# Reversed column order in the three-pass float32r products of an attention, mixer and mixture kernel

## The chip, the cores and the metric

The kernel runs on one core of a Trainium2 chip. The metric is the device time of one execution in microseconds, as the median of the runs shown. One further execution was taken with the hardware profiler, and all rows below come from it.

## The reference, cut to what matters

Three stages follow one another, for a batch of 4, a sequence of 448 and a model width of 768 (12 heads of 64):

```python
q_n, k_n = rmsnorm(q, g_q), rmsnorm(k, g_k)             # stage 1, per head
attn = softmax(q_n @ k_n.T / 8);  x = attn @ v
h  = relu(x.T @ w_tok1) @ w_tok2                        # stage 2, over the sequence
u  = x + h.T
u  = u + relu(u @ w_ch1) @ w_ch2                        # over the channels, 768 -> 1536 -> 768
for e in range(4):                                      # stage 3, causal attention experts
    ye = softmax(mask(q_e @ k_e.T / 8)) @ v_e @ wo[e]   # q_e, k_e, v_e = u @ wq[e], wk[e], wv[e]
    out += gate_e(u) * ye                               # top 2 of 4 by u @ w_gate
```

All inputs and the output are float32.

## The kernel before, in words

**Two kinds of matrix product.** The score products (line 577), the products with v (line 643) and the transposes (lines 603, 620, 658) take float32 operands. The dense products, which are those with the token weights, the channel weights, the expert projections and the output weights, go through the helpers `product` and `mm3`. There each operand is held as two float32r halves, a rounded one (index 0) and the rest (index 1), side by side in a tile of shape [128, 2, width]. `mm3` multiplies in three passes, (0,0), (1,0) and (0,1) of stationary half and moving half, each one matmul (line 508) that adds to the same row of PSUM. All of these have 128 stationary columns, or 112 for the values of the experts. The moving operand has 448 columns, in 2,304 passes; 260 columns for the values with the gate, in 288; and 256 columns in the first token product, in 288. The output row in PSUM has as many columns and is contiguous, as the moving operand is.

**What feeds and follows them.** A weight tile (`whl`, ring of 6) is split into its halves on ScalarE and VectorE or POOL the first time it is needed, written to a DRAM copy (`kept`) and fetched from there for the later batches (line 499). `narrow` unpacks the raw weights, with reads that take every second 32-bit word (lines 453 and 456, and `half` in 458 and 460). The moving operands `uhl`, `hid`, `xhl` and the second halves are written by ScalarE (lines 419, 424) and VectorE (lines 425, 438, 918, 951). After the last pass of a product ScalarE or VectorE reads the finished PSUM row (lines 419, 424, 934, 951, 962); each reads it by one instruction over the whole row.

**Order of the work.** All steps are collected by a planner (`Plan`) that lays them out on a model of the engines: `product` gives it a cost of three times `pass_ns(n)` for three passes, and the order so found is issued as it is. The two PSUM rows of a ring (`ps_a`, `ps_m`, `ps_s`, two buffers each) and the SBUF rings (`RING`) bound how far it runs ahead. The tags in `SHIFT` get 64 bytes of padding ahead of their ring. Attention pairs of one batch are interleaved with the dense products of the batch before, so that ScalarE's exponentials and VectorE's row maxima (lines 562 and 552) have TensorE work beside them.

Of the kernel before, what the change touches and what calls it, by code (L numbers as in the profile page):

```python
# [308 lines left out]
def kernel(  # L309
# [196 lines left out]
    def mm3(acc, lhs, rhs, first, last):  # L506
        for i, (x, y) in enumerate(PASSES):
            nc.tensor.matmul(  # L508
                acc, lhs[:, x], rhs[:, y], start=first and i == 0, stop=last and i == 2
            )  # L510

    def product(acc, pa, terms, n, more=False):

        m = len(terms)
        for i, (reads, lhs, rhs) in enumerate(terms):
            add("PE", 3 * pass_ns(n), reads, [pa],
                lambda i=i, lhs=lhs, rhs=rhs: mm3(
                    acc(), lhs(), rhs(), i == 0, i == m - 1 and not more))
# [632 lines left out]
```

## Time and profile before

| what | value |
|---|---|
| median of 3 runs | 908.91 us (907.31 to 909.79) |
| span of the profiled execution | 903.5 us (its page gives no other time of its own) |
| TensorE matmul busy | 874.8 us, 97% |
| weight load busy (overlaps the matmuls) | 690.0 us, 76% |
| VectorE, ScalarE, POOL busy | 527.4, 441.7, 55.1 us |
| data moved by DMA | 163.28 MB, 181 GB/s |

The span runs from the first to the last instruction; a timed run is some microseconds longer. A matmul's duration in the rows is that of one instruction from its start to the end of its results, and matmuls overlap, so the time of a stream of them is read from the starts: the time between two starts, divided by the number of matmuls between.

### The profile page before, as it was taken

How to read it: one execution, taken by the hardware profiler on the slowest of the kernel's cores; microseconds unless marked ns; L12 is line 12 of the kernel's file. 1: busy time of each engine (PE TensorE's matmuls, PEld its weight loads, DVE VectorE, ACT ScalarE, POOL GpSimd, SP SyncE). 2: the span in 40 equal slices, each digit the busy share in tenths (PEclk: the TensorE clock that was granted, in tenths of full speed). 3: DMA queues.
4: the chain of work that ended last, by engine and by line, in shares of the span. 5: the costliest groups of instructions: out<-in, count | busy, mean ns of one | idle time of the engine just before them, and what ended most of it. 6: DMA issues, size and time to landing. Idle time of an engine off the chain costs nothing.

```text
span 903.5 us, 14257 instructions
## 1 busy us (share of the span) xinstructions
PE 874.8 (97%) x5160; PEld 690.0 (76%) x5160; DVE 527.4 (58%) x1154; ACT 441.7 (49%) x1047; POOL 55.1 (6%) x68
## 2 busy tenths in 40 slices
PE   3899999999999999999999999999999999999998
PEld 1445688777778878868778787887777799998886
DVE  7998999899984964453452574443363282124342
ACT  5898856767763553344244345144434440004453
POOL 1014001020100200000000010000000010001000
PEclk9999999999999999999999999999999999999999
DMA  7755868787779538846355406764453225675334
GB/s 203 199 172 171 236 222 270 246 264 261 240 261 246 171 108 243 255 150 206 104 161 148 157 21 177 223 209 156 121 169 109 62 80 175 222 232 173 111 128 169
DMA packets 103223, 163.28 MB, mean 181 GB/s; under 512 B 14096, under 2 KB 70288, under 8 KB 103152
## 3 DMA queue, kind: packets, MB, share of 16 engines
q1 hardware_dynamic: 103008, 162.36, 58.2%
q8 instruction: 41, 0.67, 0.3%
q14 instruction: 30, 0.25, 0.1%
q10 hardware_dynamic: 144, 0.00, 0.0%
HBM read 131.55 MB, written 30.77 MB: 180 GB/s over the span
## 4 chain that ended last, share of the span: by engine, by line
PE 87%; DVE 5%; ACT 5%; DMA 1%; issue 1%; ACTq 0%; DVEq 0%; SPq 0%
PE a L508 56%; PE s L577 10%; PE m L643 9%; PE s L620 7%; PE m L658 3%; ACT s L562 2%; DVE nm L552 1%; DMA nat<-in_nat_dram 1%; PE s L582 1%; PE a L603 1%; ACT s L419 1%; DVE st L755 1%; ACT wraw L453 0%; ACT w L456 0%; DVE s L420 0%
## 5 line engine op out<-in xcount | busy, mean ns | idle before, releaser
L508 PE MATMUL a<-uhl,whl 128*128 128x448 f32 x1152 | 246.4, 366 | 1.1 <-DVE whl L438 0.6
L508 PEld LDWEIGHTS a<-uhl,whl 128*128 128x128 f32 x1152 | 212.5, 188 | 27.9 <-issue 9.4
L508 PE MATMUL a<-hid,whl 128*128 128x448 f32 x864 | 190.1, 368 | 0.0
L562 ACT ACTIVATE s<-s,nm,st 112x448 f32<-112x448 f32 x192 | 137.2, 726 | 101.5 <-DVE nm L556 59.9
L508 PEld LDWEIGHTS a<-hid,whl 128*128 128x128 f32 x864 | 158.2, 188 | 22.9 <-issue 9.5
L552 DVE TENSOR_REDUCE nm<-s 112x2 f32<-112x896 f32 (+3 forms) x128 | 125.9, 998 | 73.0 <-PE s L577 40.3
L577 PE MATMUL s<-k,q 64*112 64x448 f32 (+3 forms) x512 | 109.7, 543 | 5.7 <-ACT s L562 4.9
L419 ACT ACTIVATE s<-s 112x896 f32<-112x896 f32 (+3 forms) x121 | 78.9, 696 | 53.3 <-PE s L620 49.4
L962 DVE TENSOR_TENSOR u<-a,u 128x448 f32<-128x448 f32 x72 | 44.6, 622 | 72.6 <-PE a L508 72.2
L620 PE MATMUL s<-ident,s 112*112 112x112 f32 x736 | 81.9, 259 | 0.0
L620 PEld LDWEIGHTS s<-ident,s 112*112 112x112 f32 x736 | 75.0, 133 | 5.3 <-issue 0.7
L424 ACT ACTIVATE hid<-a 128x448 fp32r<-128x448 f32 x42 | 22.9, 544 | 112.6 <-PE a L508 112.5
L643 PE MATMUL m<-s,v 112*64 112x448 f32 x384 | 77.2, 545 | 0.0
L577 PEld LDWEIGHTS s<-k,q 64*112 64x112 f32 x512 | 39.6, 177 | 46.0 <-issue 28.7
L951 DVE SCALAR_TENSOR_TENSOR hid<-a,hid 128x448 fp32r<-128x448 f32 x48 | 29.8, 622 | 75.8 <-ACT hid L424 75.8
L643 PEld LDWEIGHTS m<-s,v 112*64 112x64 f32 x384 | 25.5, 136 | 41.5 <-issue 39.5
L562 ACT ACTIVATE s<-s,nm 112x112 f32<-112x112 f32 (+3 forms) x64 | 30.9, 493 | 39.7 <-DVE nm L552 39.4
L562 ACT ACTIVATION_READ_ACCUMULATOR s<-s,nm,st 112x1 f32 x192 | 39.3, 204 | 0.0
L508 PE MATMUL a<-whl,uhl 128*112 128x260 f32 x288 | 39.0, 287 | 0.0
L508 PE MATMUL a<-xhl,t 112*128 112x256 f32 x288 | 37.9, 284 | 0.6 <-ACT s L419 0.3
L508 PEld LDWEIGHTS a<-whl,uhl 128*112 128x112 f32 x288 | 35.5, 175 | 2.2 <-issue 1.4
L508 PEld LDWEIGHTS a<-xhl,t 112*128 112x128 f32 x288 | 34.8, 188 | 2.8 <-issue 1.4
(123 smaller groups left out, 906.5 us busy)
## 6 DMA issues: line engine op xcount, KB each, us to landing
whl<-kept_c SPq DMA_DIRECT2D x72, 384.0 KB, 4.1
whl<-kept_c SPq DMA_DIRECT2D x108, 256.0 KB, 3.2
w<-in_wc_dram SPq DMA_DIRECT2D x24, 384.0 KB, 4.1
kept_c<-whl SPq DMA_DIRECT2D x24, 384.0 KB, 4.1
w<-in_wc_dram SPq DMA_DIRECT2D x36, 256.0 KB, 3.2
kept_c<-whl SPq DMA_DIRECT2D x36, 256.0 KB, 3.7
whl<-kept_qk SPq DMA_DIRECT2D x24, 384.0 KB, 3.5
nat<-in_nat_dram SPq DMA_DIRECT2D x19, 448.0 KB, 4.6
```

What stands on the lines that cost most here:

```text
L419: lambda e: nc.scalar.activation(dst(), src(), AF.Copy) if e == "ACT"
L424: lambda e: nc.scalar.activation(dst(), src(), AF.Relu) if e == "ACT"
L508: nc.tensor.matmul(acc, lhs[:, x], rhs[:, y], start=first and i == 0, stop=last and i == 2)
L552: lambda e: e.tensor_reduce(nm.t[:, c], pst.t[:CP, :, :w], axis=AX.X, op=ALU.max, negate=True))
L562: lambda j=j: nc.scalar.activation(s[j].t[:, c, :w], pst.t[:CP, j, :w], AF.Exp, bias=nm.t[:, c, j : j + 1], scale=1.0 if rq is None else r ...
L577: nc.tensor.matmul(pst.t[:CP, j, :w], q.t[me, CP * c : CP * c + CP], k.t[me, :w], start=True, stop=not causal)
L582: nc.tensor.matmul(pst.t[:CP, j, width[c] - CP : width[c]], eye, veil, start=False, stop=True)
L620: nc.tensor.transpose(pst.t[:CP, c - cc, CP * r : CP * r + CP], s.t[:, r, CP * c : CP * c + CP], ident[:CP, :CP])
L643: nc.tensor.matmul(av.t[64 * j : 64 * j + 64, q0:S], vat(j, c)[1](), p.t[:, c, q0:], start=c == 0, stop=c == NCH - 1)
L658: nc.tensor.transpose(dst(c), src(c), ident[:p, :p])
L951: lambda e, hl=hl, pa=pa: e.scalar_tensor_tensor(hl.t[:, 1], pa.t[:, :S], 0.0, f(hl.t[:, 0]), op0=ALU.max, op1=ALU.subtract))
L962: dve(S, [pa], [u], lambda e, u=u, pa=pa: e.tensor_add(u.t, pa.t[:, :S], u.t))
```

## The change

Both the moving operand and the PSUM row of `mm3` are given with a step of minus one in the column dimension. The last column is read first and written first, to the last place of the row, so every column's sum goes where it went. The stationary operand, the order of the passes, the flags, all other matmuls, the planner and its costs stay.

```diff
     def mm3(acc, lhs, rhs, first, last):
         for i, (x, y) in enumerate(PASSES):
             nc.tensor.matmul(
-                acc, lhs[:, x], rhs[:, y], start=first and i == 0, stop=last and i == 2
+                acc[:, ::-1], lhs[:, x], rhs[:, y][:, ::-1],
+                start=first and i == 0, stop=last and i == 2,
             )
```

## Rows read from the trace of the kernel before

**Rows 1.** The page, busy time of each engine: us (share of the span) xinstructions.
```profile
PE 874.8 (97%) x5160; PEld 690.0 (76%) x5160; DVE 527.4 (58%) x1154; ACT 441.7 (49%) x1047; POOL 55.1 (6%) x68
```
**Rows 2.** The page, chain that ended last: shares by engine, then by line.
```profile
PE 87%; DVE 5%; ACT 5%; DMA 1%; issue 1%; ACTq 0%; DVEq 0%; SPq 0%
...
PE a L508 56%; PE s L577 10%; PE m L643 9%; PE s L620 7%; PE m L658 3%; ACT s L562 2%; DVE nm L552 1%; DMA nat<-in_nat_dram 1%; PE s L582 1%; PE a L603 1%; ACT s L419 1%; DVE st L755 1%; ACT wraw L453 0%; ACT w L456 0%; DVE s L420 0%
```
**Rows 3.** Windows, all instructions: window, length, busy of five engines, PEclk, DMA share, GB/s.
```profile
0.00:25.00 25.00, 9.42 (x31) 3.69 (x32) 19.25 (x51) 14.75 (x32) 3.14 (x10) 0.93 0.67 191
...
150.00:300.00 150.00, 149.44 (x882) 113.19 (x880) 123.44 (x289) 98.49 (x242) 17.50 (x18) 1.00 0.82 258
...
660.00:800.00 140.00, 140.00 (x823) 119.85 (x822) 53.69 (x118) 38.91 (x85) 3.86 (x5) 1.00 0.46 144
```
**Rows 4.** Waits of PE for other engines: total us, times, longest (three longest of 14).
```profile
PE m L658 <- DVE st L758: 9.8, 1, 9.8
PE s L577 <- ACT s L562: 4.9, 4, 2.9
PE a L603 <- ACT s L419: 2.3, 8, 0.6
```
**Rows 5.** PE in order of time, 740.8 to 817: start, us, operation xcount.
```profile
743.24 14.56 PE L508 MATMUL a<-uhl,whl 128*128 128x448 f32 x72
757.64 14.56 PE L508 MATMUL a<-hid,whl 128*128 128x448 f32 x72
772.04 14.56 PE L508 MATMUL a<-uhl,whl 128*128 128x448 f32 x72
786.44 14.56 PE L508 MATMUL a<-hid,whl 128*128 128x448 f32 x72
800.84 14.56 PE L508 MATMUL a<-uhl,whl 128*128 128x448 f32 x72
```
**Rows 6.** PE in order of time, the narrow passes and what starts after them.
```profile
280.08 4.58 PE L508 MATMUL a<-whl,uhl 128*112 128x260 f32 x36
284.49 0.74 PE L620 MATMUL s<-ident,s 112*112 112x112 f32 x6
...
304.40 1.65 PE L508 MATMUL a<-xhl,t 112*128 112x256 f32 x12
305.88 0.83 PE L620 MATMUL s<-ident,s 112*112 112x112 f32 x7
```
**Rows 7.** Line 508 by itself: duration min/median/max ns of matmuls and weight loads.
```profile
L508 PEld LDWEIGHTS a<-uhl,whl x1152: 186/188/192, 118.0 to 859.6; 128*128 128x128 f32 x192
L508 PE MATMUL a<-uhl,whl x1152: 360/363/476, 118.0 to 859.8; 128*128 128x448 f32 x192
```
**Rows 8.** Chain in order of time: one float32 product with v, 8 matmuls in 16 records.
```profile
34.48 3.16 PE m L643 x16
```
**Rows 9.** ScalarE groups: reads of every second word (L453), then contiguous reads (L419).
```profile
L453 ACT ACTIVATE wraw<-w 128x384 f32<-128x384 f32 x24 | 13.4, 559 | 5.5 <-DMA w<-in_wc_dram 3.7 <-DVE nm L552 1.8
...
L419 ACT ACTIVATE whl<-wraw 128x384 fp32r<-128x384 f32 x10 | 5.4, 536 | 8.6 <-DVE wraw L460 6.0 <-PE a L508 2.6
```

## The prediction

> **What bounds the kernel now.** The first view is the busy time of the engines: TensorE's matmuls are busy for 874.8 of 903.5 us, and no other engine passes 58% [rows 1]. The second is the chain that ended last: 87% of it is TensorE, and line 508 alone, the three-pass products, is 56%, some 506 us [rows 2]. The third are windows along the span: from about 150 us on TensorE is busy for practically every microsecond, also where the DMA engines have their highest share (149.44 of 150 us beside a DMA share of 0.82); only the first 25 us, which hold no line 508 work worth counting, are a stage of waits on others [rows 3]. The largest wait of a matmul for another engine is 9.8 us, once, on the statistics at the start; the next is 4.9 us in four pieces [rows 4]. So TensorE's own rate is the bound. What a pass of line 508 gains or loses reaches the end nearly one to one, and the only question is what a pass costs with its columns in the other order.
>
> That cost is read from the starts in an undisturbed stretch near the end. Seventy-two passes begin at 743.24 and the next seventy-two at 757.64: 14.40 us / 72 = 200.0 ns per pass of 448 columns, and the same in each of the four intervals [rows 5]. The granted clock there is 1.00, so 2.4 GHz [rows 3]; one column per cycle would be 448 / 2.4 = 186.7 ns. A pass thus takes 13.3 ns beyond its columns. For the narrow passes: 36 of 260 columns from 280.08 to 284.49, 122.5 ns each against 108.3 for the columns alone; 12 of 256 columns from 304.40 to 305.88, 123.3 ns against 106.7, each with the turn to another kind of work in it [rows 6]. The stream is limited by columns; the weight load, 188 ns each, fits under a pass of 200 [rows 7].
>
> **The change part by part.** No instruction is added, removed or moved. The planner's costs aren't touched, so the issue order, the DMAs, the rings and the waits stay. The two halves of a moving operand stay apart in the reversed form, and the consumers read whole rows after the last pass, so it is of no use or harm to them which column was written first. What changes is the inside of 2,304 + 288 + 288 = 2,880 matmuls: the order in which TensorE reads SBUF and writes PSUM.
>
> 1. *The moving read, step minus one.* The trace has no negative step on any engine. Nearest row: ScalarE reading every second word of 384 takes 559 ns against 536 for contiguous words, 4% more [rows 9]. That instruction is slower per column than TensorE, so it shows only that a step other than one isn't punished by itself. The lower end is a gain of all that a pass has beyond its columns: 13.3 x 2,304 = 30.6 us, 14.2 x 288 = 4.1 us and 16.6 x 288 = 4.8 us, together 39.5 us. The upper end: each column takes twice its time. The nearest row for a matmul that handles 448 columns at such a rate is the float32 product with v, 8 matmuls in 3.16 us or 395 ns each [rows 8]. By it a pass costs 195 ns more: 195 x 2,304 = 449 us; a narrow pass of about 258 columns would be 395 x 258 / 448 = 227 ns, 104 more than its 123, x 576 = 60 us; together 509 us.
> 2. *The PSUM write, step minus one.* Read and write run in the same stream, so the slower sets the pass; the ends are the same two, and they are not added.
>
> I take 0 for both. The reversed stream touches the same words, four bytes apart, one neighbour after the other, and the one row with another step is 4% from the contiguous one, far nearer to none than to twice. The sum by the profiled execution is 903.5 + 0 = 903.5 us of span. The runs' median lies 908.91 - 903.5 = 5.4 us above that span; this part (start and end of an execution) isn't touched, so the forecast is 908.9 us. What this kernel's timing can tell from no change is about 0.3%, 2.7 us; shared over 2,880 passes that is 0.95 ns per pass. The forecast of no change is therefore a narrow one: a pass between 199.1 and 200.9 ns.
>
> The rule that speaks against the change is the Trainium skill's, in Advanced Engine Details and Errata, section Memory Cachelines: SBUF is accessed in lines of 16 bytes and PSUM in lines of 8, two float32 values, and a non-contiguous pattern in PSUM slows matmuls markedly. If a descending row counts as non-contiguous there, the sum would be the one of the second rival below; if only the line counts, two neighbours in descending order still share one and the sum stays. No run here shows which.
>
> **The rivals.**
>
> *A. A pass gets shorter, and the kernel faster.* The 13.3 ns beyond the columns may be cycles in which the moving read and the read of the next weights, which runs at the same time in SBUF, disturb each other. Reversing one of the two streams alters how they meet. For it: weight loads are busy beside the matmuls for 76% of the span [rows 1]. Against it: nearly the same excess stands on passes of 448, 260 and 256 columns (13.3, 14.2, 16.6 ns) [rows 5, 6], which looks like a fixed step per matmul, and a step like that doesn't care for the order. All of it gone is 39.5 us: 869.4 us; half of it 889 us. With TensorE faster, the next thing late would be the weight fetches in the 150 to 300 us window, where the DMA engines are already at 0.82 [rows 3]; 7% less time would put them at 0.88, still under the whole. The skill's page TensorE: Matmul & The Clock Gate, section Step-by-step, gives the weights and the moving operand two separate read ports of SBUF, so that a weight load takes nothing from the running matmul; by that the gain would be 0. The trace doesn't contradict it and doesn't prove it.
>
> *B. Each column takes twice its time (slower).* Place: the PSUM write, or the SBUF read, of the 2,880 passes. If neighbours are only taken together in ascending order, a reversed row is handled one column at a time. Point from which it decides: at 2.4 GHz a column has 0.42 ns; as soon as one descending column needs more, every pass is bound by it, and nothing hides it, since TensorE is the bound already. Price as in part 1: 509 us, or 908.9 + 509 = 1,418 us by the nearest row; by exact doubling of the columns (186.7 x 2,304 + 107.5 x 576 = 492 us) 1,401 us. Against it stands only that the words are neighbours all the same; no row of a reversed operand speaks for or against.
>
> *C. The same disturbance as in A, but more of it (slower).* If the order makes the two streams meet more often, an excess that doubles costs what A would win: 908.9 + 39.5 = 948 us, half of that 929 us.
>
> *D. The change doesn't do what it says:* a matmul with a reversed operand runs in the slower float32 form, with its operands taken twice. At two matmul records for each pass, as line 643 has, and each column at twice its time, it would be far past B, some 2 x 395 = 790 ns per pass of 448 columns, above 2,200 us. Nothing in the profile speaks for it.
>
> **How the numbers follow.** No change within 0.3%: 0.43. A: 0.20, most of it near half of the excess. C: 0.14. B: 0.20. D: 0.03. Faster is A, 0.20; within 0.3% is 0.43; slower is B, C and D, 0.37. Cases of both signs and one with a price of half the kernel hold most of the chance together, so the range is wide: it leaves out D, and the part of A in which over 60% of the excess goes, and reaches up to B's price: 884 to 1,420 us. The likeliest case has a range of its own of 906.2 to 911.6 us.
>
> **What would show each step.** In the profile of the changed kernel I expect the five starts of the long stretch again 14.40 us apart for 72 passes, the median matmul at 363 ns, the weight load at 188 ns, the matmuls' busy share at 97%, and the same count of instructions. Under A or C those intervals move by up to 0.96 us per 72 while the float32 lines (577, 620, 643) keep their durations, and the excess changes more on rows of 448 than on 256. Under B they become 27 to 28 us, line 508 rises from 56% of the chain to over 70%, and VectorE and ScalarE fall below 40% and 33% of a span of 1,400 us at unchanged busy time. Under D line 508 has twice its records. The prediction is wrong if a pass of the long stretch differs from 200.0 ns by over 1 ns, or if a wait appears at line 508 that rows 4 don't have, such as on the second half of `hid`.

## The result, and the profile after

The changed kernel takes 919.54 us (918.92 to 921.79, 4 runs) against 908.11 us (906.15 to 909.79, 4 runs) for the kernel before: a ratio of 1.0134, with a 95% interval of 1.0114 to 1.0155. It is slower by about 11.4 us. The forecast was no change, 908.9 us. The direction is that of rival C, at a little over half of C's smaller price.

The page after, busy time of the engines, against rows 1:

```profile
PE 887.8 (97%) x5160; PEld 691.7 (75%) x5160; DVE 527.9 (58%) x1154; ACT 442.9 (48%) x1047; POOL 54.8 (6%) x68
```

The counts are the same on every engine. TensorE's matmuls are busy for 13.0 us more, and no other row here moved by more than 1.7 us. TensorE in order of time in the long stretch, against rows 5:

```profile
753.98 15.04 PE L508 MATMUL a<-uhl,whl 128*128 128x448 f32 x72
768.86 15.04 PE L508 MATMUL a<-hid,whl 128*128 128x448 f32 x72
783.74 15.04 PE L508 MATMUL a<-uhl,whl 128*128 128x448 f32 x72
798.62 15.04 PE L508 MATMUL a<-hid,whl 128*128 128x448 f32 x72
813.50 15.04 PE L508 MATMUL a<-uhl,whl 128*128 128x448 f32 x72
```

The starts are 14.88 us apart in each of the four intervals, so 206.7 ns a pass where [rows 5] gave 200.0. The granted clock there is 1.00 again, as the windows after show (columns as in rows 3):

```profile
660.00:800.00 140.00, 140.00 (x818) 117.17 (x815) 56.19 (x125) 43.54 (x95) 3.83 (x5) 1.00 0.42 132
```

Line 508 by itself, against rows 7, and then the 260-column passes in order of time, against rows 6:

```profile
L508 PEld LDWEIGHTS a<-uhl,whl x1152: 186/188/192, 118.9 to 873.5; 128*128 128x128 f32 x192
L508 PE MATMUL a<-uhl,whl x1152: 366/368/476, 118.9 to 873.7; 128*128 128x448 f32 x192
```

```profile
283.56 4.57 PE L508 MATMUL a<-whl,uhl 128*112 128x260 f32 x36
287.97 1.12 PE L621 MATMUL s<-ident,s 112*112 112x112 f32 x10
```

A matmul of 448 columns lasts 368 ns and not 363; the weight load still lasts 188 ns; the 36 passes of 260 columns again take (287.97 - 283.56) / 36 = 122.5 ns.

Where the time went can be added up, since both kernels issue the same matmuls in the same order. From the first to the last matmul start the trace before spans 889.7 us and the trace after 903.4 us, 13.6 us more. Of these, 2,173 intervals between two successive passes of 448 columns hold 12.2 us (5.6 ns each in the mean; those at a turn between kinds of work change less), 269 intervals between passes of 256 columns hold 0.5 us (2.0 ns each), 269 of 260 columns hold 0.0 us, and the longer gaps beside all these under 1 us. The first matmul starts 0.6 us later. That makes the 14.2 us between the spans of 917.7 and 903.5 us. The medians lie 11.4 us apart: the run whose span is 917.7 us took 919.54 us, 1.8 us more, so the profiled execution of before would have been a run of about 905.3 us, faster than its median.

The largest wait of a matmul is still the one at the start:

```profile
PE m L659 <- DVE st L759: 10.4, 1, 10.4
```

### The profile page after: what moved, and what is told of

The parts are those of the page before. It is cut to its first block, busy times and chain, and to the rows that moved or that the text cites. A ratio compares the mean times of both kernels' runs of the same rounds, so it can differ in the third digit from the quotient of the medians.

```text
span 917.7 us, 14271 instructions
## 1 busy us (share of the span) xinstructions
PE 887.8 (97%) x5160; PEld 691.7 (75%) x5160; DVE 527.9 (58%) x1154; ACT 442.9 (48%) x1047; POOL 54.8 (6%) x68
## 4 chain that ended last, share of the span: by engine, by line
PE 85%; DVE 5%; ACT 4%; DMA 4%; issue 1%; SPq 0%; ACTq 0%; DVEq 0%
PE a L508 55%; PE s L578 10%; PE m L644 9%; PE s L621 7%; PE m L659 3%; ACT s L563 2%; DMA nat<-in_nat_dram 1%; DMA rs<-st 1%; PE a L604 1%; PE s L583 1%; DVE nm L553 1%; ACT s L419 1%; DMA whl<-kept_c 1%; DMA out_dram<-ot 0%; DVE st L756 0%
## 5 line engine op out<-in xcount | busy, mean ns | idle before, releaser
L508 PE MATMUL a<-uhl,whl 128*128 128x448 f32 x1152 | 253.3, 372 | 1.0 <-ACT ot L419 0.4
L508 PE MATMUL a<-hid,whl 128*128 128x448 f32 x864 | 195.1, 373 | 0.5 <-DMA whl<-kept_c 0.5
L419 ACT ACTIVATE s<-s 112x896 f32<-112x896 f32 (+3 forms) x121 | 78.8, 696 | 55.8 <-PE s L621 51.9
L578 PEld LDWEIGHTS s<-k,q 64*112 64x112 f32 x512 | 39.5, 176 | 46.1 <-issue 28.2
L458 DVE SCALAR_TENSOR_TENSOR wraw<-wraw,w 128x256 uint32<-128x256 uint32 (+3 forms) x72 | 32.9, 457 | 8.2 <-ACT w L456 5.5
```

The source lines that it names most:

```text
L419: lambda e: nc.scalar.activation(dst(), src(), AF.Copy) if e == "ACT"
L458: dve(n, [(d, 0)], [(r, part)], lambda e: e.scalar_tensor_tensor(ru(), ru(), 3, half(0), op0=ALU.logical_shift_left, op1=ALU.bitwise_or), ...
L508: nc.tensor.matmul(acc[:, ::-1], lhs[:, x], rhs[:, y][:, ::-1], start=first and i == 0, stop=last and i == 2,)
L578: nc.tensor.matmul(pst.t[:CP, j, :w], q.t[me, CP * c : CP * c + CP], k.t[me, :w], start=True, stop=not causal)
```

## The experiments

**One side of the change at a time.** In the first only the moving read is reversed, in the second only the PSUM write.

```diff
-                acc[:, ::-1], lhs[:, x], rhs[:, y][:, ::-1],
+                acc, lhs[:, x], rhs[:, y][:, ::-1],          # e1
+                acc[:, ::-1], lhs[:, x], rhs[:, y],          # e2
```

> Only the moving operand is read from its last column to its first; the PSUM row is written first to last, so each product's columns come out mirrored (its time is what is asked for). Theory R (the extra time arises where the moving operand is read from SBUF, beside the read of the next weights): a pass of 448 columns takes the changed kernel's 206.7 ns, 72 passes 14.88 us, the whole about 919.5 us. Theory W (it arises where the row is written to PSUM, for instance because two neighbours are only taken together in ascending order): 200.0 ns, 14.40 us, the whole about 908 us. If both sides share in it: between the two.

> Only the PSUM row is written from its last place to its first; the moving operand is read first to last, so each product's columns come out mirrored. Theory R: 200.0 ns a pass, 14.40 us for 72, the whole about 908 us. Theory W: 206.7 ns, 14.88 us, about 919.5 us.

TensorE in order of time in the same stretch, first with the reversed read, then with the reversed write:

```profile
770.27 15.04 PE L508 MATMUL a<-hid,whl 128*128 128x448 f32 x72
785.15 15.04 PE L508 MATMUL a<-uhl,whl 128*128 128x448 f32 x72
800.03 15.04 PE L508 MATMUL a<-hid,whl 128*128 128x448 f32 x72
```

```profile
758.68 14.56 PE L508 MATMUL a<-hid,whl 128*128 128x448 f32 x72
773.08 14.56 PE L508 MATMUL a<-uhl,whl 128*128 128x448 f32 x72
787.48 14.56 PE L508 MATMUL a<-hid,whl 128*128 128x448 f32 x72
```

With the read alone the intervals are 14.88 us and the time is 918.53 us, a ratio of 1.0128 (1.0098 to 1.0157). With the write alone they are 14.40 us and the time is 906.9 us, a ratio of 1.0008 (0.9995 to 1.0022). Theory W falls: the whole of the loss belongs to the moving read, and a PSUM row written from its last place to its first costs nothing that can be measured.

**All weights from one column.** The 128 stationary columns are read from one word of each partition (step zero), ascending (e3) and descending (e4).

```diff
-                acc, lhs[:, x], rhs[:, y], start=first and i == 0, stop=last and i == 2
+                acc, lhs[:, x][:, 0:1].to_broadcast(list(lhs[:, x].shape)), rhs[:, y],
+                start=first and i == 0, stop=last and i == 2,
```

> The kernel before (both ascending), with the 128 stationary columns all read from the first column of their block (step zero), so that the weight load touches one word per partition and not 128; the products are not those of the reference. Theory R, in the form that the moving read and the weight read disturb each other in SBUF: the 13.3 ns beyond the columns shrink, a pass falls below 195 ns (186.7 to 190 if all of it is from there) and the whole below 896 us. A fixed step of each matmul, or theory W: 200 ns stays, the whole about 908 us.

> The changed kernel (both descending) with the same one-column weight load as the run before it; the products are not those of the reference. Theory R in the form of a disturbance between the two reads: the excess of the reversed order goes with it, a pass takes what the ascending one takes in that run, below 195 ns. If the 6.7 ns belong to a descending stream by itself, read or write: 6.7 ns above the ascending run with one weight column, so about 194 to 197 ns, or 206.7 ns if the weight read has no part in any of it.

The same stretch, ascending and then descending:

```profile
765.08 15.04 PE L508 MATMUL a<-hid,whl 128*128 128x448 f32 x72
779.96 15.07 PE L508 MATMUL a<-uhl,whl 128*128 128x448 f32 x72
794.87 15.04 PE L508 MATMUL a<-hid,whl 128*128 128x448 f32 x72
```

```profile
765.15 14.88 PE L508 MATMUL a<-hid,whl 128*128 128x448 f32 x72
779.87 14.88 PE L508 MATMUL a<-uhl,whl 128*128 128x448 f32 x72
794.59 14.88 PE L508 MATMUL a<-hid,whl 128*128 128x448 f32 x72
```

None of the expectations was met. The ascending kernel got slower (14.88 to 14.91 us, 207 ns; 915.53 us in one run beside 906.43 us) and the descending one a little faster than the changed kernel (14.72 us, 204.4 ns; 914.79 us). But the moving operand, its order and its place are the same as in the kernel before (e3) or the changed one (e4), and only the words that the weight load reads differ. So the weight read does act on the pass, and fewer words touched didn't help. Whether it acts by where it reads or by its step of zero, these two runs can't tell.

**Other places.** If place counts, the padding of `SHIFT` matters: it puts the weights 64 bytes, counted modulo 128, from the start of the moving operand, in all passes with `uhl` or `hid` as moving operand and `whl` as weights. The profile holds no addresses: this distance, here and below, is worked out from where the program's buffers lie, from the lowest address of the moving operand to the weights that are loaded during the pass. Two runs spread the six weight buffers by 32 bytes each (four floats are asked for, and the buffers end up 32 bytes further apart) and move `hid` as well:

```diff
-SHIFT = {"t1", "h1", "uhl"}
+SHIFT = {"t1": 16, "h1": 16, "uhl": 16, "hid": 24}
...
-            self.tile = self.pool.tile(
-                self.shape, self.dtype, tag=self.tag, name=self.name, bufs=self.bufs
-            )
+            flat = self.tag == "whl"
+            self.tile = self.pool.tile(
+                [128, 768 + 4] if flat else self.shape,
+                self.dtype, tag=self.tag, name=self.name, bufs=self.bufs
+            )
+            if flat:
+                self.tile = self.tile[:, :768].rearrange("p (h k) -> p h k", h=2)
```

> The kernel before with the six buffers of the weight ring 32 bytes further apart each and the ring of hid moved by 96 bytes more, so that the distance in SBUF between the moving operand and the weights that are loaded beside it takes several values in one run. Theory R-place (the cycles a pass takes beyond its columns depend on where the two streams lie in SBUF to each other): passes of 448 columns no longer all take 197 to 202 ns but fall into groups by that distance, some at 205 ns and more, some perhaps below 197. Theory R-direction (only ascending or descending counts): 200.0 ns in the mean at every distance, the whole about 907 us.

> The changed kernel with the same spread of places. Theory R-place: passes again fall into groups by the distance, other groups than in ascending order, since the reversed stream begins at another place; some reach 200 ns, and the whole lies apart from 919 us. Theory R-direction: 206.7 ns at every distance, about 919 us.

One run each gave 913.42 us ascending and 916.86 us descending, beside 906.66 us. The most frequent times of an ascending pass now range from 196 to 212 ns, those of a descending one from 201 to 211. The distance changes from pass to pass there, and the single times don't sort cleanly by it. The means do: over the whole trace an ascending pass takes 201.9 ns at 64 bytes, 203.1 at 0, 203.7 at 96 and 204.7 at 32 (315 to 565 passes each, counted as for the table below). Among the passes whose moving operand starts at one and the same place modulo 128 bytes (32), it is 201.7, 203.0, 204.8 and 204.8 ns at these four distances, so the place of the weights alone changes the pass. The distance isn't all either: at 96 bytes another place of the moving operand gives 202.8 ns and not 204.8. A descending pass takes 205.1, 206.5, 204.5 and 205.3 ns at the same four. The next runs keep the distance the same in a whole stretch. They move the ring of `uhl` and the ring of `hid` against the weights by 32-byte steps with other padding (`SHIFT` then holds the floats of padding by tag).

```diff
-SHIFT = {"t1", "h1", "uhl"}
+SHIFT = {"t1": 16, "h1": 16, "hid": 24}              # e7 ascending, e8 descending
+SHIFT = {"t1": 16, "h1": 16, "uhl": 8, "hid": 24}    # e9 descending, e10 ascending
```

> Ascending order, with the ring of uhl moved 64 bytes down (the padding of the kernel before taken out) and that of hid 32 bytes up, the weights where they are. Theory R-place: the pass leaves 200.0 ns in both stretches, by up to some 7 ns, so 14.4 to 14.9 us for 72. Theory R-direction: 14.40 us for 72 in both, the whole about 907 us.

> The changed kernel with the same two places. Theory R-place: the reversed pass leaves 206.7 ns, and at one of the places of these two runs it is back at 200 to 203 ns. Theory R-direction: 206.7 ns, 14.88 us for 72, at both places, the whole about 919 us.

> The changed kernel with uhl moved 32 bytes down and hid 64 bytes up. Theory R-place: as in the run before it, at other values; the places of hid here and of uhl there are the same modulo 128 bytes, and if the pattern repeats after 128 bytes their passes take the same time. Theory R-direction: 206.7 ns in both stretches.

> Ascending order with the places of the run before it. Theory R-place: away from 200.0 ns; if one of these two is below 200 ns the kernel before can still be beaten by a place. Theory R-direction: 200.0 ns in both stretches, the whole about 907 us.

The stretch with the distance 0 for `uhl` and 32 for `hid`, ascending and then descending:

```profile
765.50 14.95 PE L508 MATMUL a<-hid,whl 128*128 128x448 f32 x72
780.28 14.76 PE L508 MATMUL a<-uhl,whl 128*128 128x448 f32 x72
794.88 14.95 PE L508 MATMUL a<-hid,whl 128*128 128x448 f32 x72
```

```profile
770.96 15.04 PE L508 MATMUL a<-hid,whl 128*128 128x448 f32 x72
785.84 15.04 PE L508 MATMUL a<-uhl,whl 128*128 128x448 f32 x72
800.71 15.04 PE L508 MATMUL a<-hid,whl 128*128 128x448 f32 x72
```

Ascending, the same kernel now needs 14.78 us for 72 passes with `hid` and 14.60 us with `uhl`, and 914.84 us in all, 7.4 us more than before beside it, though no operand's order changed. Descending stays at 14.87 to 14.88 us, 921.59 us. The other pair gave 914.58 us ascending and 918.78 us descending beside 907.48 us.

The remaining four of the eight places 16 bytes apart were reached by starting the moving tiles 16 bytes late.

```diff
+            late = self.tag in ("uhl", "hid")
             self.tile = self.pool.tile(
-                self.shape, self.dtype, tag=self.tag, name=self.name, bufs=self.bufs
+                [128, 896 + 32] if late else self.shape,
+                self.dtype, tag=self.tag, name=self.name, bufs=self.bufs
             )
+            if late:
+                self.tile = self.tile[:, 4:900].rearrange("p (h k) -> p h k", h=2)
...
+SHIFT = {"t1": 16, "h1": 16, "uhl": 16, "hid": 8}    # e11 descending, e12 ascending
+SHIFT = {"t1": 16, "h1": 16, "uhl": 8, "hid": 24}    # e15 descending, e16 ascending
```

> The changed kernel with uhl moved by 16 bytes and hid by 48 bytes against the weights, which places in whole 32 bytes did not reach. If the reversed order has a good place at all, it is here: 200 to 203 ns a pass in one of the two stretches. If descending reads cost 206.7 ns wherever they lie: 14.88 us for 72 in both, the whole 917 to 920 us.

> Ascending order at the same two places. If the 64 bytes of the kernel before are one good place among bad ones: 203 to 207 ns a pass, the whole 913 to 918 us, so like the reversed order. If a place 16 bytes beside it is good as well or better: 200 ns or below, and the kernel before is reached or beaten.

> The changed kernel with uhl and hid at the last two of the eight places (80 and 112 bytes). If descending reads have no good place: 204.5 to 207 ns a pass in both stretches, the whole 915 to 920 us. If they have one here: 200 to 203 ns in one stretch.

> Ascending order at the same two places. If the place of the kernel before is the only good one: 203 to 206 ns a pass in both, the whole 912 to 916 us. If there is a second: 200 ns or below in one stretch.

The stretch with 48 bytes for `uhl` and 16 for `hid`, descending and then ascending:

```profile
765.87 14.96 PE L512 MATMUL a<-hid,whl 128*128 128x448 f32 x72
780.67 14.91 PE L512 MATMUL a<-uhl,whl 128*128 128x448 f32 x72
795.42 15.00 PE L512 MATMUL a<-hid,whl 128*128 128x448 f32 x72
```

```profile
763.39 14.64 PE L512 MATMUL a<-hid,whl 128*128 128x448 f32 x72
777.87 14.79 PE L512 MATMUL a<-uhl,whl 128*128 128x448 f32 x72
792.50 14.86 PE L512 MATMUL a<-hid,whl 128*128 128x448 f32 x72
```

The four runs took 916.03 (e11), 912.13 (e12), 922.38 (e15) and 914.91 us (e16), beside 908.72 us for the first two and 907.19 us for the last two. The table gives all eight places. Each number is the mean time between the starts of two successive passes with the same operands over the whole trace, 1,035 or so for `uhl` and 738 for `hid`, without the ones over 245 ns at turns between kinds of work.

| weights from moving start, modulo 128 bytes | ascending, ns | descending, ns |
|---|---|---|
| 64 (kernel before and the change) | 200.1, 200.3 | 206.6, 206.5 |
| 0 (two places modulo 256) | 203.7, 203.6 | 206.5, 206.7 |
| 16 | 203.1 | 205.9 |
| 32 | 205.3 | 206.4 |
| 48 | 202.9 | 204.8 |
| 80 | 203.9 | 204.9 |
| 96 | 204.2 | 205.3 |
| 112 | 204.2 | 205.8 |

In these runs the weights stay and only the moving operands move, so by them alone it could be the moving operand's own place that counts; e5, where the weights move too, gives the same order of the four distances. Each place but the first rests on one run in each order. Two kernels with the same reads (before and e2, the change and e1) agree in these means to 0.1 ns.

Of the eight places tried, ascending order has one good one, which the kernel before has. Descending order has none. At the seven other places descending costs 1.0 to 3.1 ns more than ascending, at this one 6.2 to 6.5 ns.

**A shorter weight load.** In the second of each three passes only 96 stationary columns are used, in the kernel before (e13) and in the changed one (e14, with both reversals kept).

```diff
+            m = 96 if i == 1 else lhs[:, x].shape[-1]
             nc.tensor.matmul(
-                acc, lhs[:, x], rhs[:, y], start=first and i == 0, stop=last and i == 2
+                acc[:m], lhs[:, x][:, :m], rhs[:, y],
+                start=first and i == 0, stop=last and i == 2,
             )
```

> The kernel before, with 96 stationary columns in place of 128 (or 112) in the second pass of each three, so that the small correction of the other rows is left out. Theory R (the excess comes from the weight load beside the moving read): three passes take less than 600 ns, by about a quarter of one pass's 13.3 ns, so 596 to 598 ns, and 72 passes 14.30 to 14.36 us. A step that belongs to each matmul whatever is loaded: 600 ns, 14.40 us.

> The changed kernel with the same 96 columns in the second pass. Theory R: three passes take less than 620 ns, by about a quarter of 20 ns, so 613 to 617 ns, 14.71 to 14.81 us for 72. If the excess is fixed: 620 ns, 14.88 us.

The stretch, ascending and then descending:

```profile
759.11 14.56 PE L509 MATMUL a<-hid,whl 128*128 128x448 f32 x72
773.51 14.56 PE L509 MATMUL a<-uhl,whl 128*128 128x448 f32 x72
787.91 14.56 PE L509 MATMUL a<-hid,whl 128*128 128x448 f32 x72
```

```profile
767.77 14.96 PE L509 MATMUL a<-hid,whl 128*128 128x448 f32 x72
782.57 14.96 PE L509 MATMUL a<-uhl,whl 128*128 128x448 f32 x72
797.37 14.96 PE L509 MATMUL a<-hid,whl 128*128 128x448 f32 x72
```

Ascending it stays at 14.40 us (906.94 us in all beside 908.72 us), as a fixed excess would; over the whole trace its passes take 201.3 to 201.4 ns in the mean, 1 ns more than in the kernel before. Descending it falls to 14.80 us (917.95 us), in the range named for theory R. The two halves disagree, so the excess isn't simply so much for each weight column loaded.

No version here beats the kernel before. The nearest that gives the kernel's own output is e12, at 912.13 us beside 908.72 us.

## Why the prediction was wrong

The time lies inside the wide range of 884 to 1,420 us, but that range reached so far up for rival B, which didn't come; the likeliest case, 906.2 to 911.6 us, and the pass of 199.1 to 200.9 ns were both missed.

- **What bounds the kernel: right.** The passes of line 508 grew, and the growth came through to the end: 13.6 us more between the first and the last matmul, and no new wait. An order of issue unchanged, counts unchanged and the longest wait at 10.4 us against 9.8 [rows 4] say the same.
- **The part that failed is step 1, "I take 0 for both".** The moving read costs 6.7 ns a pass in the long stretch, seven times the 0.95 ns that the forecast of no change allowed. It was argued from neighbouring words being touched either way and from ScalarE's 4% [rows 9]. That row says nothing of two reads at once, and the bound it gave was then taken as zero. As it came out, 206.7 / 200.0 is 3.3% more for a pass, close to that row's 4%, which was no reason to expect it.
- **The 5.4 us between span and median were misread**, without harm to the forecast. They were put down to the start and end of an execution. By the changed kernel's profiled run that part is 1.8 us; the other 3.6 us are the profiled execution of before being faster than the median.
- **Step 2, the PSUM write at no cost: right**, shown by the write alone at 1.0008. The Trainium skill's Advanced Engine Details and Errata, section Memory Cachelines, warns of non-contiguous patterns in PSUM; a descending row isn't one in this sense, by that run's 14.40 us.
- **Rival A's reason against itself was wrong.** The 13.3 ns beyond the columns was read as "a fixed step per matmul". It isn't: moving the ring of `hid` by 32 bytes took an ascending pass from 200.3 to 205.3 ns, with the same instructions in the same order. Rows of before at one placement couldn't show that; the padding in `SHIFT` was described and not weighed. The Trainium skill's TensorE: Matmul & The Clock Gate, section Step-by-step: what each phase is for, says that loading weights takes no SBUF bandwidth from the running matmul. Here another weight read beside the same moving read changes the matmul's pass by 5 to 7 ns (e3 against the kernel before), and the place of the weights alone by up to 3.1 ns (e5, 201.7 to 204.8), so the measurement disagrees with that sentence.
- **Rival C had the right direction, at 0.14.** Its reason, two reads that disturb each other, fits a pass that depends on where both lie, but no run shows how they do it. Its price was 20 us for half of the excess and 39.5 us for all. By 448-column passes half of the excess is what was added: 6.7 of 13.3 ns. The narrow passes didn't pay that share (2.0 ns on 256 columns, none on 260), nor did passes at a turn, so the sum came to 12.2 + 0.5 us, and not to 20.
- **B and D: out.** A descending column doesn't take twice its time, and there are 5,160 matmul records as before.

What the loss consists of, by the table: at the seven other places an ascending pass takes 203.9 ns in the mean and a descending one 205.7. Of the 6.4 ns that the change costs, 203.9 - 200.2 = 3.7 are the good place of the ascending order, which the reversed order doesn't have; 2.7 are left, near the 1.8 that the descending order costs in the mean elsewhere. These 2.7 are not a fixed price of descending: with one weight column the descending pass was the faster one (204.4 against 207 ns in the stretch), and in e6 a descending pass at 64 bytes took 205.1 ns and not 206.5. All this is shown as times by place; how the two reads hinder each other, and what the 13.3 ns of the good place are made of, stays open. That the stationary operand's own direction counts wasn't tried.

## What to carry to other kernels

When a kernel is bound by back-to-back matmuls, read the time between starts and subtract the columns: a rest of some nanoseconds that looks fixed may depend on where the operands lie in SBUF to each other. A placement that was found for one access order doesn't carry over to another, so a change of order is to be compared at several placements before it is judged. And a reversed operand should be tried on the read and on the write apart: here only one of them cost anything.

## What the runs showed of the hardware

- A PSUM row written from last column to first by float32r matmuls cost nothing: 1.0008 (0.9995 to 1.0022).
- Shifting the moving operand by 16 to 64 bytes against the weights changed an ascending pass of 448 columns by 2.8 to 5.0 ns, and the whole kernel by 3.4 to 7.7 us.
- In several of the slower runs the long stretch settles near one value, 14.87 to 14.91 us for 72 passes or about 206.7 ns: the changed kernel, e1, e3, e8, e9, and some intervals of e7 and e10. The others lie between, at 14.48 to 14.84 us.
- The weight load's own duration was 188 ns in the median in the kernel before, in the changed one and with one weight column: its row doesn't show that it disturbs the matmul.
